# Attention and feed-forward in one kernel: weight chunks on another DMA queue, the first loads put in order, a scale found through DRAM

## The chip, the cores and the metric

The kernel runs on one core of a Trainium2 chip. A core has a matrix engine (TensorE, "PE" in the profile, with its weight loads listed apart as "PEld"), VectorE ("DVE"), ScalarE ("ACT"), GpSimd ("POOL") and SyncE ("SP"). Each engine takes its instructions from its own list, strictly in order, and waits on semaphores for the others. DMA transfers are issued by an instruction in the list of one of these engines (here of SP or of ACT) and are then carried out by the core's DMA engines. The metric is device time in microseconds (us); before the change its median over three runs is 1113.92 us.

## The reference

Attention for 8 batches of 8 heads, 576 positions, head width 64, and then a feed-forward layer over the 4608 rows that come out of it:

```python
scores = scale * q @ k.T                       # per head, 576 x 576
cum    = cumsum(maximum(s, 0))                 # s: one number per head and position
scores = where(causal, -1e9, scores + minimum(-(cum[:, None] - cum[None, :]), 0))
attn   = softmax(scores)
x      = attn @ v                              # 4608 rows of 512 after the heads are joined
h      = x @ w_in                              # 512 x 2048
g      = where(h >= 1, h, where(h <= -1, 0, (h + 1)**2 / 4))
out    = g @ w_out                             # 2048 x 512
```

All arrays are float32, except that the host hands over the two weight matrices as 64-bit words, which the kernel decodes.

## The kernel before, in words

**Numbers.** The feed-forward products run in float16 with each operand split in two halves (high and low), three products per pair. To stay in range, everything is scaled: for each batch `batch_scales_v` (L272) finds the largest absolute value of v over all heads (`m`, the same number on all 128 partitions), from which come `ex` (the factor with which the attention output px becomes the float16 tile x), and in `batch_scales` (L282) the factors us, ws, ub, gb of the feed-forward steps. Taking a maximum over partitions needs a detour: `column_max` (L94) transposes a column of 128 numbers on TensorE against the identity matrix `ident` into PSUM (`row_m`), VectorE takes its maximum (`top_m`); `spread` (L102) makes it bfloat16 and multiplies it with a row of ones on TensorE (`col_m`), and VectorE copies that to `mb`. Both PSUM tiles come from the two buffers (pool `ps_s`) that the score tiles s and the attention outputs px rotate through.

**Weights.** Each weight matrix comes in 16 chunks of 512 KB: `Weights.load` (L179) issues one into a raw buffer (wir for w_in, four buffers; wor for w_out, four buffers in two tags). `Weights.decode` (L192) turns it into float32: ScalarE L199, VectorE L200, a TensorE product with ones for the column sums (L204), then either ScalarE L212 and VectorE L213 or VectorE L215 and L216. The load of chunk c+3 stands behind the decoding of chunk c and waits until a raw buffer is free. After four chunks `scale` (L218) makes a factor and after all 16 `split` (L225) writes the float16 halves. `a_in` (L623), the bound over all of w_in, has to be there before the first wor chunk is loaded (it is copied into the buffer, L185) and before the factors of `batch_scales(0)`.

**Attention.** A job is a pair of heads with one half of the queries (half 0: 320 queries, half 1: 256). Per job: load q and k (QF/KF for the first eight jobs, rq/rk after; `att_load`, L319), scores per query tile (L411 to L417), bias, mask and minimum on VectorE (L422), exponentials on ScalarE (L433), then `weights_t` (L439): normalise and split on GpSimd, ScalarE and VectorE (L454 to L460) and transpose through a DMA issued by SP (`pt<-pb`, L461). `att_out` (L468) multiplies with the transposed v (`vt<-vb`, L392) into px (L479) and writes x (L490, L491). Scores of the next jobs run ahead of this.

**Feed-forward.** `ffn_h` (L527): twelve products per 128 columns (L534), then L546, L549, L550 on ScalarE and VectorE and the split of g (L560, L561). `ffn_y` (L565): twelve products per 128 rows of g (L573), and for the last of them the output. The feed-forward work of one batch is woven into the attention of the next (the loop at L644).

**Start.** Lines L601 to L629: load q and k of the first job, three wir chunks, v of batch 0 and the cumulative sums (`cum_out`, L155: `cumf`, `cumd` in DRAM), then 4 jobs of attention woven with 16 chunks to decode, then the factors, three wor loads and the splits. The feed-forward of batch 0 (h, then y) is woven with the decoding of wor.

**What sets the order.** The program is written in the order above, and a scheduler that works from a model of the instructions' times rearranges each engine's list. `tc.high_priority(offset)` moves a piece ahead by that many places; `tc.issue_after(i)` ties one instruction behind another. So a change at one place can move instructions everywhere. All loads of the inputs, all transposes and the cumulative sums are issued by SP (`nc.sync`); ScalarE's queue (`nc.scalar`) carries the outputs and the sums for later jobs (`Q<-cumd`, `K<-cumd`, L360, L361).

Of the kernel before, what the change touches and what calls it, by code (L numbers as in the profile page):

```python
# [7 lines left out]
BF16 = mybir.dt.bfloat16  # L8
F16 = mybir.dt.float16
F32 = mybir.dt.float32  # L10
# [5 lines left out]
ALU = mybir.AluOpType  # L16
AX = mybir.AxisListType.X
# [3 lines left out]
B, H, S, D = 8, 8, 576, 64  # L21
DM, DFF = 512, 2048
P = 128
# [23 lines left out]
START_LEAD = 20000  # L47
# [24 lines left out]
@with_exitstack  # L72
def attention_ffn(ctx: ExitStack, tc: tile.TileContext, qT, kT, vT, s, w_in, w_out, yT):
    nc = tc.nc
    LOADQ, CUMQ = nc.sync, nc.scalar
    V, A, G, T = nc.vector, nc.scalar, nc.gpsimd, nc.tensor

    cp = ctx.enter_context(tc.tile_pool(name="cp", bufs=1))
    ap = ctx.enter_context(tc.tile_pool(name="ap", bufs=2))
    gp = ctx.enter_context(tc.tile_pool(name="gp", bufs=2))  # L80
    dp = ctx.enter_context(tc.tile_pool(name="dp", bufs=1, space=DRAM))
    ps_s = ctx.enter_context(tc.tile_pool(name="ps_s", bufs=2, space=PSUM))
# [8 lines left out]
        V.tensor_scalar(out, in_, least, None, ALU.max)  # L91
        V.tensor_scalar(out.bitcast(I32), out.bitcast(I32), 0x7F800000, None, ALU.bitwise_and)

    def column_max(src, name):  # L94

        row = ps_s.tile([P, 512], F32, tag="s", name=f"row_{name}")
        T.transpose(row[:1, :P], src, ident)
        top = ap.tile([P, 1], F32, tag="top", name=f"top_{name}")
        V.tensor_reduce(top[:1], row[:1, :P], axis=AX, op=ALU.max)
        return top[:1]  # L100

    def spread(dst, top, name):  # L102

        t16 = ap.tile([P, 1], BF16, tag="t16", name=f"t16_{name}")
        V.tensor_copy(t16[:1], top)
        col = ps_s.tile([P, 512], F32, tag="s", name=f"col_{name}")
        T.matmul(col[:, :1], ones[:1], t16[:1], start=True, stop=True)
        V.tensor_copy(dst, col[:, :1])

    BH = B * H  # L110
    KC, KF32 = D + 4, D + 2
    NQ = HALF[0][1]
    QF, KF = [], []
    for i, (tq, tk) in enumerate((("rq", "rk"), ("q1", "k1"))):
# [2 lines left out]
    one = []  # L117

    st = ap.tile([P, S], F32, tag="vraw", bufs=4, name="st")
    nc.sync.dma_start(st[:BH], s)  # L120
    ch = ap.tile([P, 2, S], F32R, tag="raw", name="ch")
    zr = ch[:BH, 1].bitcast(F32)
    V.memset(zr, 0.0)
    V.memset(QF[0][D:KF32], 8.0)
    V.memset(KF[0][D:KF32], -8.0)
    V.tensor_scalar(st[:BH], st[:BH], 0.0, None, ALU.max)
    cum = ap.tile([P, S], F32, tag="raw", name="cum")
    V.tensor_tensor_scan(cum[:BH], st[:BH], zr, 0.0, ALU.add, ALU.add)
    cumf = dp.tile([BH, S], F32, name="cumf")
    cumd = dp.tile([BH, 2, S], F32, name="cumd")  # L130

    mask = cp.tile([P, S], F32, name="mask")
    G.memset(mask, 0.0)
    G.affine_select(
        out=mask, in_=mask, pattern=[[-1, S]], compare_op=ALU.is_ge,
        fill=-8.0 * BIG, base=448, channel_multiplier=1,
# [1 line left out]

    G.memset(QF[1][D:KF32], 8.0)
    G.memset(KF[1][D:KF32], -8.0)  # L140
    ident = cp.tile([P, P], F32, name="ident")
    G.memset(ident, 0.0)
    G.affine_select(
        out=ident, in_=ident, pattern=[[-1, P]], compare_op=ALU.not_equal,
        fill=1.0, base=0, channel_multiplier=1,
    )
    ones = cp.tile([P, P], BF16, name="ones")
    G.memset(ones, 1.0)

# [19 lines left out]
    class Weights:  # L169
# [9 lines left out]
        def load(self, n, after=None):  # L179
            if n < NW:  # L180
                c = self.order[n]
                pool, tag, bufs = self.tags[n % len(self.tags)]
                self.raw[c] = pool.tile([P, NC, 2], I32, tag=tag, bufs=bufs, name=f"{self.name}r{c}")
                if after is not None:
                    V.tensor_copy(self.raw[c][:, 0, :1], after.bitcast(I32))  # L185
                src = self.src(c)
                dst = self.raw[c]
                if len(src.shape) == 4:
                    dst = dst.rearrange("p (j n) t -> p j n t", j=2)
                nc.sync.dma_start(dst, src)  # L190

        def decode(self, n):  # L192
            c, g = self.order[n], n // self.size
# [45 lines left out]
    w1 = Weights(  # L239
        "wi", lambda c: w_in[c // 4 * P:(c // 4 + 1) * P, c % 4 * NC:(c % 4 + 1) * NC, :],  # L240
        WO, WI, ((gp, "g", G_BUFS),), [n % 4 * 4 + n // 4 for n in range(NW)], 4,
    )
# [15 lines left out]
    def load_v(b):  # L258
        for p in range(NPAIR):
            v = vraw[b, p] = ap.tile([P, S], F32, tag="vraw", bufs=4, name=f"v{b}_{p}")  # L260
            nc.sync.dma_start(v, vT[b, p])
# [10 lines left out]
    def batch_scales_v(b):  # L272
        t = ap.tile([P, 1], F32, tag="mt", name=f"mt{b}")
        V.tensor_reduce(t, csc[b], axis=AX, op=ALU.max)
        m = msc[b] = ap.tile([P, 1], F32, tag="mb", name=f"mb{b}")
        spread(m, column_max(t, f"m{b}"), f"m{b}")
        r = ap.tile([P, 1], F32, tag="mr", name=f"mr{b}")
        V.reciprocal(r, m)
        e = exs[b] = ap.tile([P, NPAIR], F32, tag="ex", name=f"ex{b}")
        V.tensor_scalar(e, csc[b], r, 2.0 ** -12, ALU.mult, ALU.mult)  # L280
# [212 lines left out]
    def batch_start(b):  # L493
        batch_v(b)
        if b:
            batch_scales_v(b)
# [101 lines left out]
            ffn_y(*ffn_q.pop(0))  # L598


    att_load(0, 0)  # L601
    for c in range(3):
        w1.load(c)
    load_v(0)
    cum_out()
    batch_start(0)
    for j in range(NPAIR):
        for k in range(8):
            if k % 2 == 0:
                c = 4 * j + k // 2  # L610
# [31 lines left out]
    t = 8 * NPAIR  # L642
    tasks = w2_tasks()
    for j in range(16 * NP):  # L644
# [14 lines left out]
        else:  # L659
# [3 lines left out]
            m = 2 * (j // 8 % 2)  # L663
# [36 lines left out]
```

## Time and profile before

| | |
|---|---|
| runs (3) | 1113.92 us median, 1113.88 to 1118.03 us |
| the profiled execution | 1117.59 us, of which the span of the profile is 1115.8 us |
| busy time | PE 1013.1 us (91%), DVE 843.6 (76%), ACT 731.0 (66%), POOL 637.1 (57%) |
| DMA | 155.09 MB, 139 GB/s over the span |
| weight chunks | 16 wir and 16 wor of 512 KB, all issued by SP |

How to read it: the profile is of one execution, 3.7 us longer than the median. In rows of a timeline the first number is the start in us from the span's start, the second the duration in us, then engine, line, operation and tiles; the bracket says how long the engine sat idle before it and what ended that. "SPq" and "ACTq" are DMA issues in SP's and ACT's lists. A row of the list of waits reads "engine line <- what it waited for: us in total, times, longest". The steady part of the kernel, from about 200 us on, is bound by TensorE; before that TensorE is busy about two thirds of the time.

### The profile page before, as it was taken

The page shows a single profiled execution, that of the slowest core. Times are in us where ns is not written, and L with a number is a line of the kernel's source. Part 1 is how long each engine was busy: PE and PEld are TensorE (multiplying, and loading weights), DVE is VectorE, ACT ScalarE, POOL GpSimd, SP SyncE. Part 2 cuts the span into 40 slices and gives each one's busy share as a digit, 9 for nine tenths or more (in the row PEclk, how much of TensorE's full clock was granted, in tenths as well). Part 3 has the DMA queues.
Part 4 walks back from the last instruction along what each step waited for, and adds up shares of the span by engine and source line. Part 5 has one row for each costly group of instructions (what it writes and reads, how often), then busy time and mean ns, then how long its engine had stood idle before and what let it go on. Part 6 is the DMA issues. An engine that isn't in the chain of part 4 may idle for free.

```text
span 1115.8 us, 24709 instructions
## 1 busy us (share of the span) xinstructions
PE 1013.1 (91%) x8495; PEld 777.3 (70%) x8496; DVE 843.6 (76%) x2327; ACT 731.0 (66%) x1711; POOL 637.1 (57%) x846
## 2 busy tenths in 40 slices
PE   3558788899999999899999999899988999999998
PEld 1224456687777877787777877687767877787787
DVE  6877895787777877787877887787777888887533
ACT  4856787677576765777576765677576756776432
POOL 3555667666456664566566655556467665666422
PEclk9967889899999999999999999999999999999999
DMA  6986864776387663878377764668379663776300
GB/s 222 213 190 178 177 143 103 157 153 153 83 166 164 150 139 84 190 156 152 83 160 163 147 136 84 169 147 165 68 159 181 145 145 80 162 155 126 67 25 20
DMA packets 340925, 155.09 MB, mean 139 GB/s; under 512 B 290984, under 2 KB 322572, under 8 KB 340800
## 3 DMA queue, kind: packets, MB, share of 16 engines
q1 hardware_dynamic: 331200, 143.68, 60.2%
q10 hardware_dynamic: 9600, 9.84, 2.7%
q8 instruction: 67, 1.10, 0.4%
q14 instruction: 58, 0.48, 0.1%
HBM read 72.28 MB, written 9.88 MB: 74 GB/s over the span
## 4 chain that ended last, share of the span: by engine, by line
PE 58%; DMA 12%; DVE 11%; POOL 8%; issue 6%; ACT 4%; SPq 1%; ACTq 0%; DVEq 0%; POOLq 0%
PE h L534 25%; PE y L573 23%; DMA pt<-pb 5%; PE px L479 4%; PE s L416 3%; PE s L417 3%; DMA wir<-in_moe_w_in_dram 2%; POOL pb L457 2%; POOL pb L454 2%; DMA vt<-vb 2%; DVE pb L460 2%; DVE PS L422 1%; POOL g L561 1%; DMA wor<-in_moe_w_out_dram 1%; DVE h L549 1%
## 5 line engine op out<-in xcount | busy, mean ns | idle before, releaser
L534 PE MATMUL h<-x,WI 128*128 128x256 f16 (+1 forms) x3072 | 462.8, 292 | 8.0 <-DVE u L550 6.2
L573 PE MATMUL y<-g,WO 128*128 128x256 f16 (+1 forms) x3072 | 451.0, 288 | 9.7 <-POOL g L561 7.3
L534 PEld LDWEIGHTS <-WI 128*128 128x128 f16 x3072 | 290.3, 100 | 106.0 <-issue 21.4
L573 PEld LDWEIGHTS <-WO 128*128 128x128 f16 x3072 | 287.8, 98 | 97.0 <-issue 18.6
L561 POOL TENSOR_TENSOR g<-u,g 128x320 f16<-128x320 f32 (+1 forms) x256 | 208.6, 815 | 175.8 <-ACT g L560 175.5
L433 ACT ACTIVATE PS<-PS,mn 64x64 f32<-64x64 f32 (+4 forms) x320 | 178.8, 559 | 131.4 <-DVE mn L422 114.3
L546 ACT ACTIVATE u<-h,ub,us 128x320 f32<-128x320 f32 (+1 forms) x256 | 148.8, 582 | 116.1 <-PE h L534 100.9
L454 POOL TENSOR_SCALAR pb<-PS,rs 64x128 f16<-64x128 f32 (+4 forms) x160 | 101.0, 631 | 207.1 <-DVE rs L450 136.1
L549 DVE SCALAR_TENSOR_TENSOR h<-h,ws,u 128x320 f32<-128x320 f32 (+1 forms) x256 | 132.3, 518 | 107.8 <-ACT u L546 106.5
L457 POOL TENSOR_TENSOR pb<-PS,pb 64x128 f16<-64x128 f32 (+4 forms) x160 | 168.0, 1050 | 11.5
L460 DVE SCALAR_TENSOR_TENSOR pb<-PS,rs,pb 64x128 f16<-64x128 f32 (+4 forms) x160 | 135.1, 845 | 49.6 <-POOL pb L454 49.0
L422 DVE CUSTOM_DVE_ANT_0 PS<-s,mask 64x64 f32<-64x64 f32 (+4 forms) x320 | 133.3, 419 | 26.3 <-PE s L417 23.4
L550 DVE SCALAR_TENSOR_TENSOR u<-u,r,h 128x320 f32<-128x320 f32 (+1 forms) x256 | 130.0, 508 | 6.6
L416 PE MATMUL s<-K,Q 128*64 128x64 f32 (+1 forms) x336 | 126.3, 378 | 6.2 <-DVE mn L422 2.6
L455 ACT ACTIVATE PS<-PS,rs 64x64 f32<-64x64 f32 (+4 forms) x160 | 88.9, 559 | 49.2 <-DVE rs L450 49.1
L560 ACT CAST g<-u 128x320 f16<-128x320 f32 (+1 forms) x256 | 107.9, 422 | 13.5 <-DVE u L550 13.4
L417 PE MATMUL s<-K,Q 68*64 68x64 f32 (+1 forms) x336 | 102.8, 309 | 7.2 <-POOL K L367 4.3
L479 PEld LDWEIGHTS <-vt 128*64 128x64 f16 x1536 | 73.5, 114 | 49.2 <-issue 37.2
L479 PE MATMUL px<-pt,vt 128*64 128x256 f16 (+3 forms) x1536 | 83.4, 259 | 23.7 <-DMA pt<-pb 20.9
L456 POOL TENSOR_SCALAR pb<-PS 64x128 f16<-64x128 f32 (+4 forms) x160 | 90.5, 566 | 21.0 <-ACT PS L455 19.0
L416 PEld LDWEIGHTS s<-K,Q 128*64 128x64 f32 (+1 forms) x336 | 61.5, 183 | 17.1 <-DVE mn L422 3.2
L417 PEld LDWEIGHTS s<-K,Q 68*64 68x64 f32 (+1 forms) x336 | 61.9, 185 | 9.5 <-POOL K L367 4.4
(108 smaller groups left out, 930.3 us busy)
## 6 DMA issues: line engine op xcount, KB each, us to landing
rk<-in_k_dram SPq DMA_DIRECT2D x56, 288.0 KB
v<-in_v_dram SPq DMA_DIRECT2D x32, 288.0 KB
rq<-in_q_dram SPq DMA_DIRECT2D x56, 160.0 KB
rk<-in_k_dram SPq DMA_DIRECT2D x56, 160.0 KB
wir<-in_moe_w_in_dram SPq DMA_DIRECT2D x16, 512.0 KB
wor<-in_moe_w_out_dram SPq DMA_DIRECT2D x16, 512.0 KB
rq<-in_q_dram SPq DMA_DIRECT2D x56, 128.0 KB
out_dram<-o ACTq DMA_DIRECT2D x32, 160.0 KB
```

The source lines that it names most:

```text
L416: T.matmul(sc[:R, :c1 - c0], Q1[:, hd, qo:qo + R], K1[:, hd, c0:c1], start=True, stop=False)
L417: T.matmul(sc[:R, :c1 - c0], Q2[:KC, hd, qo:qo + R], K2[:KC, hd, c0:c1], start=False, stop=True)
L422: ttr[0] = V.tensor_tensor_reduce(out=Pt[:R, c0:c1], in0=sc[:R, :c1 - c0], in1=mask[:R, mo:mo + c1 - c0], scale=-0.125 if j < F32_JOBS els ...
L433: A.activation(Pt[:R, :W], Pt[:R, :W], AF.Exp, bias=m2[:R], scale=-1.0, accum_out=sums[n, i][:R, hd:hd + 1])
L457: G.tensor_tensor(los[1], pw, his[1], ALU.subtract)
L460: V.scalar_tensor_tensor(los[0], pv, rs[:R, :1], his[0], ALU.mult, ALU.subtract)
L479: T.matmul(px[hd * D:(hd + 1) * D, lo:N], VT[:, vl * NB + j, hd * D:(hd + 1) * D], PT[:, 4 * j + 2 * hd + pl, lo:], start=(m == 0), stop=( ...
L534: T.matmul(h[:, :N], WI[4 * kt + ft // 4][:, wl, ft % 4 * P:(ft % 4 + 1) * P], x[:, kt, xl], start=(n == 0), stop=(n == 3 * NKT - 1),)
L546: first = A.activation(u, h[:, :N], AF.Relu, bias=ubi[b], scale=usc[b][:, fg:fg + 1]).ins
L549: V.scalar_tensor_tensor(h[:, :N], h[:, :N], wsc[b][:, fg:fg + 1], u, ALU.mult, ALU.max)
L561: G.tensor_tensor(g[:, 1], u, g[:, 0], ALU.subtract)
L573: T.matmul(ys[b, hf, m][:, :N], WO[8 * (m // 2) + ft // 2][:, wl, c0:c0 + P], g[:, gl], start=(ft == 0 and n == 0), stop=(ft == NFT - 1 an ...
```

## The change

Three edits, and what the scheduler makes of them.

```diff
@@ queue of the weight chunks
-    LOADQ, CUMQ = nc.sync, nc.scalar
+    LOADQ, CUMQ, WQ = nc.sync, nc.scalar, nc.scalar
...
-                nc.sync.dma_start(dst, src)
+                WQ.dma_start(dst, src)

@@ s, the sums, and first q, k put first
-    nc.sync.dma_start(st[:BH], s)
...
+    with tc.high_priority(offset=2 * START_LEAD):
+        nc.sync.dma_start(st[:BH], s)
+        V.memset(QF[0][D:KF32], 8.0)
+        zr = ch[:BH, 1].bitcast(F32)
+        V.memset(zr, 0.0)
+        V.memset(KF[0][D:KF32], -8.0)
+        V.tensor_scalar(st[:BH], st[:BH], 0.0, None, ALU.max)
+        V.tensor_tensor_scan(cum[:BH], st[:BH], zr, 0.0, ALU.add, ALU.add)
...
-    att_load(0, 0)
-    for c in range(3):
-        w1.load(c)
+    with tc.high_priority(offset=2 * START_LEAD):
+        for c in range(3):
+            w1.load(c)
+        att_load(0, 0)

@@ the largest value through DRAM (batch_scales_v)
         V.tensor_reduce(t, csc[b], axis=AX, op=ALU.max)
+        d = dp.tile([P], F32, name=f"md{b}")
+        nc.sync.dma_start(d.rearrange("(p o) -> p o", o=1), t)
+        a = ap.tile([P, P], F32, tag="ma", bufs=1, name=f"ma{b}")
+        nc.sync.dma_start(a, d.partition_broadcast(P))
         m = msc[b] = ap.tile([P, 1], F32, tag="mb", name=f"mb{b}")
-        spread(m, column_max(t, f"m{b}"), f"m{b}")
+        V.tensor_reduce(m, a, axis=AX, op=ALU.max)
```

`column_max`, `spread` and `ident` (a memset and an affine_select on GpSimd at the start) are gone. All 32 weight chunks are now issued from ScalarE's list. The column t of 128 numbers is written to DRAM (`md`) by one DMA of SP, read back by a second one as 128 equal rows (`ma`), and one VectorE maximum over each row gives `mb`.

**The start.** SP's list before, from its first load to the third wir chunk (lines of the kernel before; QF0/KF0 are q and k of the first job):

```order
L328 DMA QF1_79<-in_q_dram 64x2x320
L328 DMA KF1_80<-in_k_dram 64x2x320
L120 DMA st_81<-in_s_dram 64x576
L328 DMA QF0_77<-in_q_dram 64x2x320
L328 DMA KF0_78<-in_k_dram 64x2x320
L190 DMA wir0_161<-in_moe_w_in_dram 128x1024
L190 DMA wir4_163<-in_moe_w_in_dram 128x1024
L190 DMA wir8_165<-in_moe_w_in_dram 128x1024
```

After these rows come ten more DMAs (four rows of the sums, the four v, cumf, cumd), and only then the fourth chunk, wir12.

ACT's list now, from its first row (L169 is the changed kernel's line of the load, L178 and L191 are the decoding):

```order
L169 DMA wir0_150<-in_moe_w_in_dram 128x1024
L169 DMA wir4_152<-in_moe_w_in_dram 128x1024
L169 DMA wir8_154<-in_moe_w_in_dram 128x1024
L169 DMA wir12_190<-in_moe_w_in_dram 128x1024
L178 ACT_TABLE_LOAD
L178 ACTIVATE WO0_121<-wir0_150 128x512
L191 ACTIVATE wir0_150<-wir0_150,floor_bias_75 128x512
L178 ACTIVATE WO4_125<-wir4_152 128x512
L169 DMA wir1_202<-in_moe_w_in_dram 128x1024
```

Four chunks stand at the head of ACT's list where three stood behind five loads on SP, and the fourth no longer stands behind the ten DMAs. SP's list now begins with st, QF0, KF0, QF1.

**The first feed-forward step.** ACT's list around x of the fourth job (px3) and the first u (L546 before, L529 now). Before:

```order
L229 ACTIVATE WI15_125<-WO15_141,r_wi_145 128x512
L199 ACTIVATE WO2_128<-wor0_740 128x512
L490 ACTIVATE x0_0_440<-px3_0_699,ex0_297 128x320
L212 ACTIVATE wor0_740<-wor0_740,floor_bias_75 128x512
L199 ACTIVATE WO3_129<-wor1_743 128x512
L433 ACTIVATE PS512_151,sm0_3_852<-PS512_151,mn0_3_0_0_855 128x448
L199 ACTIVATE WO4_130<-wor2_746 128x512
L546 ACTIVATE u0_0_0_815<-h0_0_0_801,ub0_735,us0_731 128x320
```

Three wor chunks are begun ahead of the first u. Now, in the changed kernel's ACT list at the same place:

```order
L169 DMA wor9_912<-in_moe_w_out_dram 128x2x512
L178 ACTIVATE WO9_130<-wor7_854 128x512
L473 ACTIVATE x0_0_431<-px3_0_690,ex0_288 128x320
L178 ACTIVATE WO10_131<-wor8_861 128x512
L191 ACTIVATE wor8_861<-wor8_861,floor_bias_75 128x512
L178 ACTIVATE WO11_132<-wor9_912 128x512
L416 ACTIVATE PS512_146,sm0_3_843<-PS512_146,mn0_3_0_0_846 128x448
L529 ACTIVATE u0_0_0_806<-h0_0_0_792,ub0_726,us0_722 128x320
```

Before, one wor chunk is begun ahead of that x and three ahead of the first u; now eight (wor0 to wor7) and ten.

**The scale of a batch.** DVE's list at batch 3 in the changed kernel, from the column of maxima (mt) to the result (mb); L532 and L533 are the feed-forward steps (L549 and L550 before):

```order
L253 TENSOR_REDUCE mt3_5298<-c3_5288 128x1
L432 TENSOR_SCALAR rs11_4_5353<-sm11_4_5255 128x2
L249 TENSOR_SCALAR rc3_5289<-rc3_5289 128x4
L532 SCALAR_TENSOR_TENSOR h2_0_8_5412<-h2_0_8_5412,ws2_4447,u2_0_8_5426 128x320
L433 RECIPROCAL rs11_4_5353<-rs11_4_5353 128x2
L533 SCALAR_TENSOR_TENSOR u2_0_8_5426<-u2_0_8_5426,r2_4437,h2_0_8_5412 128x320
L405 ISA PS128_144,mn12_0_0_0_5451<-s12_0_0_0_5448,mask_92 64x64
L405 ISA mn12_0_0_0_5451 64x1
L474 SCALAR_TENSOR_TENSOR x2_1_4896<-px10_1_5360,ex2_3400,x2_1_4896 128x256
L443 SCALAR_TENSOR_TENSOR pb11_4_5352<-PS640_148,rs11_4_5353,pb11_4_5352 128x5x128
L259 TENSOR_REDUCE mb3_5304<-ma3_5302 128x1
L532 SCALAR_TENSOR_TENSOR h2_0_9_5456<-h2_0_9_5456,ws2_4447,u2_0_9_5469 128x320
```

Nine rows stand between mt and mb; before, eight stood there, among them `top_m` and its cast. In batch 1 it is four rows now, in batch 0 twenty-four.

More of the change, by code (lines that the diff above doesn't have):

```diff
@@ L92, in pow2floor @@
         V.tensor_scalar(out.bitcast(I32), out.bitcast(I32), 0x7F800000, None, ALU.bitwise_and)
[L94 to L108, printed above, removed]
     BH = B * H
@@ L119, in attention_ffn @@
     st = ap.tile([P, S], F32, tag="vraw", bufs=4, name="st")
-    nc.sync.dma_start(st[:BH], s)
     ch = ap.tile([P, 2, S], F32R, tag="raw", name="ch")
[L122 to L126, printed above, removed]
     cum = ap.tile([P, S], F32, tag="raw", name="cum")
-    V.tensor_tensor_scan(cum[:BH], st[:BH], zr, 0.0, ALU.add, ALU.add)
     cumf = dp.tile([BH, S], F32, name="cumf")
     cumd = dp.tile([BH, 2, S], F32, name="cumd")
+    with tc.high_priority(offset=2 * START_LEAD):
[6 more added lines that the diff above has]
+        V.tensor_tensor_scan(cum[:BH], st[:BH], zr, 0.0, ALU.add, ALU.add)
     mask = cp.tile([P, S], F32, name="mask")
@@ L140, in attention_ffn @@
     G.memset(KF[1][D:KF32], -8.0)
[L141 to L146, printed above, removed]
     ones = cp.tile([P, P], BF16, name="ones")
```

## The prediction

> **What bounds the kernel now.** I read the page first, then a table of stages, the waits and the chain of the start. The page says that TensorE is busy nine tenths of the time:
>
> ```profile
> span 1115.8 us, 24709 instructions
> PE 1013.1 (91%) x8495; PEld 777.3 (70%) x8496; DVE 843.6 (76%) x2327; ACT 731.0 (66%) x1711; POOL 637.1 (57%) x846
> ```
>
> That is a mean over two different stages. In the table of stages the columns are the stretch in us, its length, the busy time of PE, PEld, DVE, ACT and POOL (instructions behind an x), the granted TensorE clock, the DMA engines' busy share and GB/s:
>
> ```profile
> 0.00:20.00 20.00, 5.17 (x13) 2.40 (x13) 14.11 (x35) 7.34 (x12) 7.49 (x18) 1.00 0.80 242
> 20.00:60.00 40.00, 21.68 (x80) 10.61 (x80) 32.51 (x96) 32.29 (x68) 20.07 (x29) 1.00 0.78 192
> 60.00:90.00 30.00, 14.55 (x65) 8.46 (x66) 19.72 (x69) 14.85 (x34) 18.68 (x24) 0.53 0.88 217
> 130.00:160.00 30.00, 26.49 (x158) 15.90 (x157) 26.69 (x56) 28.33 (x54) 21.30 (x20) 0.90 0.80 170
> 200.00:1116.00 916.00, 881.05 (x7750) 697.19 (x7750) 693.91 (x1916) 594.47 (x1439) 522.44 (x708) 0.99 0.62 131
> 0.00:160.00 160.00, 99.37 (x473) 56.34 (x475) 126.68 (x336) 110.01 (x218) 86.74 (x109) 0.84 0.78 195
> ```
>
> From 200 us on TensorE is busy for 881 of 916 us (96%): what is saved on another engine there is worth nothing unless TensorE waits for it. In the first 160 us TensorE is idle for 60.6 us, VectorE for 33.3 and ScalarE for 50.0. The start is therefore where time can be found. What it waits for, over these 160 us:
>
> ```profile
> PE sum_wi L204 <- DVE WO L200: 24.3, 10, 10.4
> ACT WO L199 <- DMA wir<-in_moe_w_in_dram: 18.0, 7, 7.2
> DVE WO L200 <- ACT WO L199: 14.5, 11, 4.3
> PE px L479 <- DMA pt<-pb: 10.9, 3, 7.4
> ACT WO L199 <- DMA wor<-in_moe_w_out_dram: 8.8, 6, 3.4
> ```
>
> ScalarE waits 26.8 us for weight chunks, VectorE behind it 14.5 us, TensorE behind both. In the chain of waits of the first 100 us the longest DMA pieces say the same (start, length, what); the row of SP's timeline below them shows why the first is long:
>
> ```profile
> 13.62 8.25 DMA wir<-in_moe_w_in_dram
> 37.53 7.14 DMA pt<-pb
> 71.76 5.56 DMA wir<-in_moe_w_in_dram
> 84.68 4.44 DMA wor<-in_moe_w_out_dram
> ```
>
> ```profile
> 13.62 2.50 SPq L190 DMA_DIRECT2D wir<-in_moe_w_in_dram  x3
> ```
>
> The fourth chunk is issued only at 13.62 us, because SP's list has the sums and v ahead of it.
>
> **The change part by part.** *Start: queue and order.* Four chunks now head ACT's list, so the fourth comes some 12 us earlier, and later chunks no longer wait in SP's list behind transposes. The part of VectorE's idle time that wir chunks caused is one row of what waits for the tile wir:
>
> ```profile
>   DVE WO L200: 8.8, 7
> ```
>
> The other 5.7 of the 14.5 us are behind wor chunks. Can the DMA engines deliver earlier? From 0 to 90 us they are free for 0.20 x 20 + 0.22 x 40 + 0.12 x 30 = 16.4 us, so there is room for 8.8 us, not for much more.
>
> But the order costs something too. Three points of the start, the bound over w_in, x of the fourth job and the first feed-forward step on VectorE, with the durations of decoding (mean ns behind the busy time) and the stage table's row up to 109 us:
>
> ```profile
> 82.55 0.14 DVE L623 TENSOR_REDUCE a_in<-bound_wi 128x1 f32<-128x4 f32 x1
> 89.77 0.51 ACT L490 ACTIVATE x<-px,ex 128x320 f16<-128x320 f32 x1
> 93.79 1.07 DVE L549 SCALAR_TENSOR_TENSOR h<-h,ws,u 128x320 f32<-128x320 f32 x2
> L200 DVE TENSOR_SCALAR WO<-WO 128x512 int32<-128x512 int32 x31 | 15.9, 514 | 14.5 <-ACT WO L199 14.5
> L213 DVE SCALAR_TENSOR_TENSOR WO<-wor,WO 128x512 int32<-128x512 int32 x8 | 6.8, 850 | 1.6 <-ACT wor L212 1.6
> L216 DVE SCALAR_TENSOR_TENSOR WO<-wor,WO 128x512 int32<-128x512 int32 x7 | 5.9, 845 | 0.0
> L215 DVE SCALAR_TENSOR_TENSOR WO<-wor,WO 128x512 int32<-128x512 int32 x7 | 5.4, 771 | 0.0
> 90.00:93.80 3.80, 3.47 (x9) 1.77 (x9) 2.87 (x8) 3.80 (x8) 1.43 (x2) 0.50 0.24 93
> 90.00:109.00 19.00, 17.40 (x73) 9.89 (x73) 16.72 (x42) 15.30 (x29) 7.69 (x9) 0.76 0.43 140
> ```
>
> Ahead of that step VectorE's new list has seven more L200, three more L213 and four more each of L215 and L216: 3.6 + 2.6 + 3.1 + 3.4 = 12.6 us, with small ones 13. Before, VectorE had worked 66.3 + 2.9 = 69.2 us when it got there at 93.8 and had been idle 24.6. Now it has 82.2 us to do first; with 8.8 us less idle it gets there at 82.2 + 15.8 = 98.0. Later than before, but before, 82 us of work were reached only at 108 to 109 us (66.3 + 16.7 = 83.0 at 109). In work done the lead is 8.8 us, and up to 10. The weights allow it: 8.8 us less puts `a_in` at 73.8, or sooner since part of the fourth job's work now stands behind it; the first chunk takes 4.4 us, nine more at 0.52 MB and 217 GB/s take 2.4 each, which ends at 99.8, about the same time. I take **-7 us**: the 8.8, less some 2 us because x now stands behind eight chunks. Bounds: -14.5 (wor waits too) and +11 (rival C).
>
> *ScalarE issues the chunks.* Each issue takes, on SP, as a view of line L190 has it (min/median/max ns):
>
> ```profile
> L190 SPq DMA_DIRECT2D wir<-in_moe_w_in_dram x16: 357/392/1340, 4.1 to 71.8; - x16
> L190 SPq DMA_DIRECT2D wor<-in_moe_w_out_dram x16: 368/405/537, 84.7 to 150.8; - x16
> ```
>
> 16 x 0.39 + 16 x 0.41 = 12.8 us on ScalarE. It lies in ScalarE's 50 us of idle time, except where ScalarE is full (28.3 of 30 us at 130 to 160), where a few issues fall: **+1 us**; bounds 0 and 12.8 if that cover is gone. An issue also waits for VectorE to free its buffer, with exponentials behind it; in the new list the instruction behind nearly always waits for a later VectorE result anyway, so nothing for that.
>
> *The detour through TensorE goes.* Eight times (min/median/max ns):
>
> ```profile
> L97 PE MATMUL row_m<-ident,mt x8: 272/273/373, 20.3 to 920.6; 128*1 128x128 f32 x8
> L107 PE MATMUL col_m<-t_m,ones x8: 172/172/179, 25.0 to 924.1; 1*128 1x1 bf16 x8
> ```
>
> Seven of the eight are in the stage where TensorE is full: 7 x 0.445 = 3.1 us, **-3 us**. VectorE loses a reduction, a cast and a copy and gains a reduction: nothing. GpSimd's identity matrix goes from a time when GpSimd next waits for VectorE: nothing.
>
> *The trip through DRAM comes.* mb now follows mt by two DMAs in series. No row shows such a trip; the nearest are a DMA of 1.2 KB that TensorE waits for and the write of 144 KB to DRAM that the next load waits for. Beside them mt and mb before, in batch 2:
>
> ```profile
> 9.76 0.59 SPq L333 DMA_DIRECT2D KF<-cum  x1
> 12.42 0.58 PE L204 MATMUL sum_wi<-WO,ones 128*128 128x512 bf16 x1 [1.48 <-DMA KF<-cum]
> 12.44 0.50 SPq L156 DMA_DIRECT2D cumf<-cum  x1
> 16.80 0.68 SPq L336 DMA_DIRECT2D QF<-cumf  x1
> 296.60 0.12 DVE L274 TENSOR_REDUCE mt<-c 128x1 f32<-128x4 f32 x1
> 303.16 0.15 DVE L108 COPY mb<-col_m 128x1 f32<-128x1 f32 x1
> ```
>
> So 2.7 to 4.4 us each, 5.4 to 8.8 for two, against 6.6 us before. VectorE, with feed-forward and score steps queued behind mb, comes out between 1.2 us sooner and 2.2 us later at each of seven boundaries (batch 0's has 24 rows of cover); SP holds a transpose and loads of the next job behind ma. A gain I exclude, since TensorE's waits there do not name mb; the loss is at most 15 us. TensorE has h and y products queued, so I take a small part, nearest to the middle of the rows: **+2 us**. If the cover were gone it would be the 15.
>
> Sum: -7 + 1 - 3 + 2 = -7. The profiled execution took 1117.6 us (span 1115.8), which gives 1110.6; it was 3.7 us above the median, so the median should be **1107 us**.
>
> **The rivals.**
> *A, the transposes gain too.* The 7.14 us of the chain at 37.5 are a transpose behind 2 MB of weights on the same queue. On its own queue it would not stand behind them: half of the 10.9 us that px waits for pt goes as well, and the trip costs nothing: -8.8 - 5 - 3 + 1 = -16, 1098 us. For it: free DMA time; against: the same engines carry both, and weights could as well get ahead of the transposes. Chance 0.17.
> *B, the queue moves nothing.* The DMA engines are busy for 0.78 to 0.88 of the start, and a chunk that comes earlier makes q, k, v or a transpose later by as much; the wait changes its name. The start gives at most 1 us, and with -3, +1 and +2 the result is 1117.6 - 1 - 3.7 = 1113 us. Chance 0.22. The Trainium skill, "DMA: Bandwidth & Descriptors", section "Issuing engines are not separate DMA queues", says this as a rule: transfers from different issuers run on the same 16 engines and interleave, and issuing from several saves only the sequencer's time. The trace agrees as far as the shares go, but 13.62 us for the fourth chunk is an issue that comes late, which the rule leaves room for; that is why I do not put it first.
> *C, the first feed-forward step is late (slower).* On ScalarE x of job four waits behind eight wor chunks, u behind ten. If `a_in` stays near 82.6, the chunks end at 84.7 + 4.4 + 9 x 2.4 = 110.7, 17.6 us after the first u now (93.2); 12.6 us of decoding are then done ahead, so 5 us are lost, and at 3.4 us per chunk 14. With -3 + 1 + 2 that is +5 to +14: 1119 to 1128, say 1122 us. It decides if `a_in` comes after about 78 us. Chance 0.11.
> *D, the trip stalls VectorE (slower).* The 15 us in full on TensorE, with the start's gain: -7 + 1 - 3 + 15 = +6, 1120 us. Against it: TensorE's queue of products. Chance 0.05.
>
> **How the numbers follow.** Forecast 0.45, with a range of its own from 1102 to 1111; A 0.17, B 0.22, C 0.11, D 0.05. Some 0.5% (5.6 us) is what a measurement here can tell from no change. Faster than 1108.3: 0.31 of the forecast, A, and 0.04 of B, 0.52. Within: 0.14 of the forecast, 0.17 of B, 0.31. Slower than 1119.5: C, D and a little of B, 0.17. The range from 1097 to 1120 leaves out part of A below, and half of C and D above.
>
> **What would show it.** Right: the fourth wir chunk decoded by 16 us rather than 21.9; ScalarE's wait for wir under 10 us; `a_in` at 66 to 75; first u at 95 to 101; VectorE idle in the first 160 us down by about 7; wor finished some 20 us earlier; PE full from about 160. Wrong: `a_in` after 78 (B or C); ScalarE's waits for wor grown beyond 20 us (C); VectorE waiting over 2 us for ma at each boundary with TensorE idle beside it (D); TensorE's idle time after 200 us changed by more than 5 us either way, which a new order of the steady part could do and no term here holds.

## The result and the profile after

The changed kernel takes 1170.39 us (median of four runs, 1162.22 to 1178.9), beside 1114.27 us for the kernel before on the same chip: a ratio of 1.050, with a 95% interval from 1.045 to 1.055. 1107 us were forecast, so it is 56 us slower where 7 us less were expected. The profiled execution took 1178.9 us, 61 us more than that of before. TensorE's work is the same, spread over a longer span:

```profile
span 1177.1 us, 24685 instructions
PE 1014.8 (86%) x8480; PEld 775.7 (66%) x8480; DVE 833.7 (71%) x2311; ACT 733.5 (62%) x1711; POOL 632.3 (54%) x844
```

The table of stages, with the columns of before, and below it before's row for 100 to 160 us:

```profile
20.00:60.00 40.00, 10.83 (x42) 5.45 (x41) 25.55 (x79) 21.59 (x42) 13.19 (x17) 1.00 0.99 173
100.00:160.00 60.00, 34.76 (x165) 19.21 (x164) 42.04 (x90) 38.53 (x67) 25.64 (x28) 0.96 0.71 164
0.00:160.00 160.00, 71.45 (x297) 38.87 (x298) 109.81 (x287) 96.48 (x183) 69.32 (x89) 0.99 0.83 177
200.00:1116.00 916.00, 846.32 (x7400) 661.29 (x7398) 674.04 (x1913) 585.14 (x1421) 514.61 (x701) 0.96 0.62 134
```

```profile
100.00:160.00 60.00, 48.30 (x286) 29.67 (x286) 51.98 (x119) 47.40 (x91) 38.29 (x37) 0.89 0.81 185
```

The loss lies in both stages. In the first 160 us TensorE is busy for 71.5 us, 28 less than before (297 matmul records instead of 473). Of that, 10.9 us are lost from 20 to 60 us (10.8 against 21.7), where the DMA engines are busy all the time (0.99) and yet move less (173 GB/s; 0.78 and 192 before), and 13.5 us from 100 to 160 us, with 121 of the 176 missing records. From 200 to 1116 us TensorE is busy for 846 us, 35 less. The steady part has a wait that was not there, in the lists of waits of VectorE and of TensorE from 200 us on:

```profile
DVE mb L259 <- DMA ma<-md: 60.3, 7, 12.3
PE s L399 <- DVE mn L405: 34.5, 7, 8.5
```

One boundary, the last, in the timelines of VectorE, SP and TensorE (sorted by start):

```profile
968.50 0.13 DVE L253 TENSOR_REDUCE mt<-c 128x1 f32<-128x4 f32 x1
969.11 0.59 SPq L255 DMA_DIRECT2D md<-mt  x1
976.40 0.33 SPq L257 DMA_DIRECT2D ma<-md  x1
980.49 0.29 DVE L259 TENSOR_REDUCE mb<-ma 128x1 f32<-128x128 f32 x1 [7.75 <-DMA ma<-md]
981.41 0.53 PE L399 MATMUL s<-K,Q 128*128 128x192 f32 x1 [5.75 <-DVE mn L405]
982.22 2.56 SPq L444 DMA_TRANSPOSE pt<-pb  x1
```

The write of 128 numbers to DRAM takes 7.3 us (from md's issue to ma's, with only two other issues of SP between; 7.1 to 8.9 us at the seven boundaries), the read 4 us. mb is 12 us behind mt; VectorE has about 4 us of work to put between and stands for 7.8 us; the next scores stand behind it on TensorE.

The start, first in milestones (ScalarE's decoding of the fourth chunk, the bound over w_in, x of the fourth job, the first u), then the longer DMA pieces of the chain of waits up to 124 us (two of wir, at 51.65 and 63.01, are left out), and ScalarE's wait for wor chunks in the first 160 us:

```profile
13.60 0.69 ACT L178 ACTIVATE WO<-wir 128x512 f32<-128x512 f32 x1
L607 DVE TENSOR_REDUCE a_in<-bound_wi x1: 131/131/131, 80.4 to 80.4; 128x1 f32<-128x4 f32 x1
124.03 0.53 ACT L473 ACTIVATE x<-px,ex 128x320 f16<-128x320 f32 x1 [1.32 <-PE px L462]
127.58 0.59 ACT L529 ACTIVATE u<-h,ub,us 128x320 f32<-128x320 f32 x1
```

```profile
2.87 9.95 DMA QF<-in_q_dram
14.76 10.47 DMA cumf<-cum
32.09 12.57 DMA md<-mt
44.68 5.70 DMA ma<-md
81.52 13.09 DMA pt<-pb
98.51 3.83 DMA wor<-in_moe_w_out_dram
102.42 5.95 DMA wor<-in_moe_w_out_dram
108.53 4.34 DMA wor<-in_moe_w_out_dram
112.98 9.32 DMA wor<-in_moe_w_out_dram
ACT WO L178 <- DMA wor<-in_moe_w_out_dram: 21.9, 8, 7.0
```

The fourth chunk is there at 13.6 us instead of 21.9, as forecast. But the bound over w_in comes at 80.4 (82.5 before, 66 to 75 forecast), x of the fourth job at 124.0 (89.8) and the first u at 127.6 (93.2). SP's own transfers in the start are slow now: in the chain q of the second job takes 10 us, the sums 10.5 us, a transpose 13.1 us, and batch 0's trip through DRAM 18.3 us. What stands behind ma cannot leave SP's list before 44.7 us, among it a load of q and a transpose:

```profile
45.10 0.68 SPq L311 DMA_DIRECT2D QF<-in_q_dram  x1
47.95 1.21 SPq L444 DMA_TRANSPOSE pt<-pb  x1
```

From 98.5 us to x of the fourth job the chain is mostly four loads of wor chunks, 23.4 us together: eight of these chunks stand ahead of that x in ScalarE's list, and in the first 160 us ScalarE waits 21.9 us for wor chunks (8.8 before). This is the stretch from 100 us on in which most of the matmuls are missing.

### The profile page after: what moved, and what is told of

The parts are those of the page before. It is cut to its first block, busy times and chain, and to the rows that moved or that the text cites. A ratio compares the mean times of both kernels' runs of the same rounds, so it can differ in the third digit from the quotient of the medians.

```text
span 1177.1 us, 24685 instructions
## 1 busy us (share of the span) xinstructions
PE 1014.8 (86%) x8480; PEld 775.7 (66%) x8480; DVE 833.7 (71%) x2311; ACT 733.5 (62%) x1711; POOL 632.3 (54%) x844
## 4 chain that ended last, share of the span: by engine, by line
PE 49%; DMA 20%; DVE 15%; issue 5%; POOL 5%; ACT 4%; SPq 0%; ACTq 0%; DVEq 0%; POOLq 0%
PE h L517 21%; PE y L556 19%; DMA md<-mt 6%; DMA vt<-vb 4%; PE px L462 4%; DMA ma<-md 3%; PE s L399 3%; PE s L400 3%; DMA wor<-in_moe_w_out_dram 2%; POOL pb L437 2%; DVE PS L405 2%; DVE h L532 2%; DVE pb L443 2%; DMA pt<-pb 1%; DVE u L533 1%
## 5 line engine op out<-in xcount | busy, mean ns | idle before, releaser
L437 POOL TENSOR_SCALAR pb<-PS,rs 64x128 f16<-64x128 f32 (+4 forms) x160 | 105.9, 662 | 258.4 <-DVE rs L433 191.4
L532 DVE SCALAR_TENSOR_TENSOR h<-h,ws,u 128x320 f32<-128x320 f32 (+1 forms) x256 | 133.0, 520 | 100.2 <-ACT u L529 99.6
L529 ACT ACTIVATE u<-h,ub,us 128x320 f32<-128x320 f32 (+1 forms) x256 | 148.7, 581 | 84.1 <-PE h L517 73.9
L440 POOL TENSOR_TENSOR pb<-PS,pb 64x128 f16<-64x128 f32 (+4 forms) x160 | 165.2, 1033 | 12.0
L399 PE MATMUL s<-K,Q 128*64 128x64 f32 (+1 forms) x336 | 128.8, 385 | 39.6 <-DVE mn L405 34.5
L533 DVE SCALAR_TENSOR_TENSOR u<-u,r,h 128x320 f32<-128x320 f32 (+1 forms) x256 | 130.5, 510 | 7.5 <-DVE h L532 0.5
L439 POOL TENSOR_SCALAR pb<-PS 64x128 f16<-64x128 f32 (+4 forms) x160 | 88.0, 550 | 5.6 <-ACT PS L438 2.4
```

The source lines that it names most:

```text
L399: T.matmul(sc[:R, :c1 - c0], Q1[:, hd, qo:qo + R], K1[:, hd, c0:c1], start=True, stop=False)
L440: G.tensor_tensor(los[1], pw, his[1], ALU.subtract)
L529: first = A.activation(u, h[:, :N], AF.Relu, bias=ubi[b], scale=usc[b][:, fg:fg + 1]).ins
L532: V.scalar_tensor_tensor(h[:, :N], h[:, :N], wsc[b][:, fg:fg + 1], u, ALU.mult, ALU.max)
```

## The experiments

Each ratio is against the kernel before, run beside it; the interval is one of 95%.

### The three edits, each alone

The third edit alone (`batch_scales_v` of the changed kernel in the kernel before):

> The kernel before with the third edit alone: the largest value goes through DRAM, weight chunks and order as before. Theory 1 (the trip holds VectorE): each trip takes 12 to 13 us from mt to mb, VectorE waits about 8 us for ma at each of seven boundaries with feed-forward and score steps behind it, TensorE loses 5 us each: 35 to 40 us, 1149 to 1154 us. Theory 2 (the boundaries lose time because the changed order of the start shifts the steady part, and the wait for ma would be hidden by itself): within 8 us of before, 1106 to 1122 us. My prediction's term was +2 - 3, that is 1113 us.

Measured: 1155.42 us, ratio 1.037 (1.032 to 1.042). This is theory 1, a microsecond above its range. From 200 to 1105 us VectorE waits for ma as in the changed kernel, and TensorE for what VectorE then brings late:

```profile
DVE mb L258 <- DMA ma<-md: 47.2, 6, 8.2
PE s L398 <- DVE mn L404: 24.3, 4, 6.4
PE h L516 <- DVE u L532: 13.9, 3, 7.2
```

These two waits of TensorE make 38 us (2.6 and 2.0 us before).

The first edit alone, and the second:

```diff
-                nc.sync.dma_start(dst, src)
+                WQ.dma_start(dst, src)        # WQ = nc.scalar
```

> The kernel before with the first edit alone: weight chunks issued by ScalarE, order and scale as before. Theory 1 (the start loses 20 to 25 us because chunks on ScalarE's queue come in ahead of transposes and q, k, and because x and u stand behind wor chunks): 1130 to 1140 us, first u after 110 us, TensorE's busy time from 0 to 200 us down by 15 or more. Theory 2 (the start loses time because batch 0's trip holds SP's list from 32 to 50 us): 1105 to 1114 us, first u before 98 us.

> The kernel before with the second edit alone: s, sums, first q, k and three chunks at high priority, all on SP. Both theories: little, as the fourth chunk still stands in SP's list: 1109 to 1118 us. A rival (the order alone costs the start, since q and k now come behind other loads on SP and the scheduler's list is new): above 1120 us.

Measured: the queue 1126.37 us, ratio 1.012 (1.007 to 1.016); the order 1115.25 us, ratio 1.001 (0.998 to 1.004). The queue loses 11 us, less than theory 1 had and not the gain of theory 2, and its first u, at 102.0 us, lies between the two as well; the order loses nothing. Queue and order together, which is the changed kernel without the trip:

> The changed kernel without its third edit: the largest value by way of TensorE as before, chunks on ScalarE's queue and the new order kept. Theory 1 (start costs 20 to 25 of its own): 1130 to 1140 us, first u after 110 us. Theory 2 (the start's loss comes from batch 0's trip): 1105 to 1112 us. If the parts add, this and the trip alone give the sum of their differences, near +56.

Measured: 1125.62 us, ratio 1.011 (1.006 to 1.015): a loss of the start's own, but about half of what theory 1 had. The parts add: 3.7 + 1.2 + 0.1 = 5.0%, as measured for all three, within intervals of 0.3 to 0.5 each.

The loss of the queue is the instructive one, since with it alone nearly everything forecast of the start came true. The bound over w_in is there at 69.4 us, in the forecast's 66 to 75, and ScalarE's wait for wir is 3.5 us (18.0 before). The first 100 us of before, of the queue alone, and of queue and order (columns as above), then two milestones of the queue alone:

```profile
0.00:100.00 100.00, 51.07 (x189) 26.67 (x190) 74.70 (x218) 62.61 (x128) 48.45 (x72) 0.81 0.77 201
```

```profile
0.00:100.00 100.00, 46.00 (x169) 22.72 (x170) 83.08 (x216) 63.83 (x125) 50.26 (x71) 1.00 0.89 225
L623 DVE TENSOR_REDUCE a_in<-bound_wi x1: 139/139/139, 69.4 to 69.4; 128x1 f32<-128x4 f32 x1
98.10 0.51 ACT L490 ACTIVATE x<-px,ex 128x320 f16<-128x320 f32 x1
```

```profile
0.00:100.00 100.00, 39.76 (x143) 21.38 (x145) 79.28 (x211) 62.95 (x123) 43.64 (x71) 1.00 0.82 211
```

VectorE has worked 83.1 us by 100 us where it had worked 74.7: a lead of 8.4 us, and the forecast said 8.8. TensorE has worked 46.0 where it had worked 51.1, and 39.8 with the order too; since the granted clock differs (0.81 before, 1.00 here), its records say it better: 169 and 143 matmuls where there were 189.

That clock makes 74.7 a poor measure, though: in this one execution of before it was 0.53 from 60 to 90 us. The trip alone, with its chunks on SP as before, had 0.97 over the first 100 us:

```profile
0.00:100.00 100.00, 54.13 (x204) 28.21 (x205) 80.91 (x224) 63.92 (x132) 51.47 (x75) 0.97 0.81 201
```

The order alone and the DMA transpose alone (below), at 1.00, have 81.6 and 78.9 us of VectorE's work and 208 and 206 matmuls. Against these three the lead is only 1.5 to 4 us, and TensorE is 35 to 39 matmuls behind. The lead is decoding; the attention of the first four jobs, on which TensorE's next work hangs, comes later.

### What stands behind the trip

The trip alone, with mb, mr and ex moved 14 slots of the attention back:

```diff
-        V.tensor_reduce(m, a, axis=AX, op=ALU.max)    # in batch_scales_v, with mr and ex
+    def batch_scales_m(b): ...                        # the same three steps
...
+            if k == 3 and j > NPAIR and n % NPAIR == 1 and hf == 0:
+                with tc.issue_after(ttr[0]):
+                    batch_scales_m(n // NPAIR)
```

> The kernel before with the trip through DRAM alone, as in the run of the trip alone, but mb, mr and ex are computed 14 slots later (some 40 rows of VectorE behind mt rather than 10). Theory 1 (the loss is VectorE standing at mb with other work behind it): the trip itself still takes 12 us, VectorE's wait for ma falls from 47 to under 5 us, the time to 1108 to 1118 us. Theory 2 (the loss is SP standing at ma, which waits for md, with loads and transposes behind it): VectorE no longer waits for ma, but the time stays above 1130 us.

Measured: 1135.67 us, ratio 1.021 (1.015 to 1.028). Both theories hold in part: from 200 us on VectorE's list of waits has no ma any more, and less than half of the loss is gone. What is left stands on SP. Three of its rows at batch 4, and the waits from 200 to 1105 us, first of before and then of this kernel:

```profile
552.21 0.59 SPq L254 DMA_DIRECT2D md<-mt  x1
559.50 0.33 SPq L256 DMA_DIRECT2D ma<-md  x1
560.59 4.10 SPq L446 DMA_TRANSPOSE pt<-pb  x1
```

```profile
POOL vb L377 <- DMA vt<-vb: 36.8, 21, 3.4
DVE pb L460 <- POOL pb L454: 44.5, 56, 3.6
PE px L479 <- DMA pt<-pb: 7.4, 5, 2.7
```

```profile
POOL vb L362 <- DMA vt<-vb: 71.2, 24, 7.5
DVE pb L445 <- POOL pb L439: 81.1, 71, 8.1
PE px L464 <- DMA pt<-pb: 13.4, 7, 4.1
```

It is still 7.3 us from md's issue to ma's; two other issues fill the first 2, then SP stands for 5.3, and the transposes of the weights and of v wait behind: GpSimd's wait for vt is twice as long, VectorE's for GpSimd nearly so, TensorE's for pt too. The same delay in the changed kernel:

> The changed kernel with mb, mr and ex computed 14 slots later. Theory 1: it falls to the time of queue and order together, 1120 to 1130 us, or a few us above it, since in the start SP still stands at ma. Theory 2: above 1140 us.

Measured: 1157.29 us, ratio 1.037 (1.031 to 1.043): 13 us less than the changed kernel, theory 2's side. Then ma's issue moved back as well, behind the next transpose of v in SP's list:

```diff
+    def batch_scales_a(b):
+        a, d = mas[b]
+        with tc.issue_after(lastturn[0]):             # the last transpose of v
+            nc.sync.dma_start(a, d.partition_broadcast(P))
```

> The kernel before with the trip alone, mb 14 slots later as in the run with the late mb, and from batch 1 on ma's issue two transposes further behind in SP's list, so that md has landed when SP comes to it. Theory 1+2 (half of the loss was VectorE standing at mb, the other half SP standing 6 to 8 us at ma with transposes behind it): 1108 to 1120 us, GpSimd's wait for vt back from 71 to 35 to 45 us. Rival (the 20 us left come from something else, the list that the scheduler makes around a later mb): it stays above 1128 us.

> The changed kernel with the same two delays, in batch 0 too. If the trip costs only by those who stand behind it, what is left is the loss of queue and order: 1118 to 1130 us. Rival: above 1140 us, the chunks on ScalarE's queue make the trip itself longer.

Measured: 1123.11 us, ratio 1.007 (1.003 to 1.011), a little above what was expected, and in the changed kernel 1133.37 us, ratio 1.015 (1.011 to 1.019), between the two figures. So of the trip's 3.7% VectorE standing at mb makes 1.6, SP standing at ma 1.4, and 0.7 are left with neither standing, each figure some 0.4 to 0.8 either way and for this order of mending; the other order was not run. In this kernel GpSimd's wait for vt is still 54.9 us, not back at 35 to 45.

### Why the trip takes 12 us

md on the other queue, ma on SP's:

```diff
-        nc.sync.dma_start(d.rearrange("(p o) -> p o", o=1), t)
+        nc.scalar.dma_start(d.rearrange("(p o) -> p o", o=1), t)
```

> The trip alone again, mb as early as in the change, but md is issued on ScalarE's queue and only ma on SP's. If md is slow because it stands behind q and k on SP's queue, the time from md's issue to ma's falls from 7 to 8 us to 3 to 4, VectorE's wait for ma to about half, and the run to 1125 to 1140 us. If a write of 128 x 4 bytes to DRAM takes that long by itself, md to ma stays at 6 to 8 us and the run at 1148 to 1158 us.

```profile
428.85 0.35 ACTq L254 DMA_DIRECT2D md<-mt  x1
436.92 0.35 SPq L256 DMA_DIRECT2D ma<-md  x1
```

Measured: 1154.36 us, ratio 1.037 (1.034 to 1.041), and 8.1 us from md to ma: the queue is not the reason. That agrees with the Trainium skill, "DMA: Bandwidth & Descriptors", section "Issuing engines are not separate DMA queues": transfers of all issuers run on the same 16 engines.

Next the form of the write. 128 pieces of 512 bytes (each partition writes its number 128 times), 4 pieces of 128 bytes (VectorE turns the column into rows of 32 first), and 128 pieces of 4 bytes that lie 512 bytes apart:

```diff
+        V.tensor_copy(w, t.to_broadcast([P, 32]))     # 4 pieces
+        V.transpose(wt, w)
+        nc.sync.dma_start(d.rearrange("(g c) -> g c", c=32), wt[::32])
...
+        d = dp.tile([P, P], F32, name=f"md{b}")       # 128 pieces, 512 bytes apart
+        nc.sync.dma_start(d[:, :1], t)
```

> The trip alone with a write of 512 bytes per partition (64 KB) in place of 4 bytes, and a read of its first row only, so that the largest value is that of partition 0: the search over partitions is left out. If the 4-byte pieces make the write slow, the time from md's issue to ma's falls from 7 to 8 us to 3 to 4 us, and the run to 1125 to 1140 us. If a write to DRAM takes that long whatever its pieces, it stays at 6 to 8 us and the run near 1155 us.

> The kernel before with the trip alone, nothing late. VectorE first turns the column of maxima into rows of 32 (a copy and a 32 x 32 transpose, under 0.5 us), so that md is written as 4 pieces of 128 bytes in place of 128 pieces of 4 bytes; ma is read as in the change and the largest value is that of all partitions. If it is the 128 small pieces that make the write take 7 to 8 us, md's issue to ma's falls to 1.5 to 3 us, VectorE's wait for ma to 10 to 20 us, and the run to 1100 to 1115 us. If any piece under 512 bytes is slow, it stays at 6 to 8 us and the run at 1148 to 1158 us.

> The trip alone with md's 128 pieces of 4 bytes written 512 bytes apart in DRAM in place of side by side, and ma read back as the first of them alone, so that the largest value is that of partition 0: the search over partitions is left out. If the write is slow because the pieces share the same few bytes' neighbourhood in DRAM, the time from md's issue to ma's falls from 7 to 8 us to 2 to 3; if it is slow because each piece is 4 bytes, it stays at 6 to 9 us.

md's issue and ma's at batch 4, of the wide write, of the four pieces, and of the spread write:

```profile
533.59 0.60 SPq L256 DMA_DIRECT2D md<-mw  x1
536.22 0.33 SPq L258 DMA_DIRECT2D ma<-md  x1
```

```profile
539.01 0.56 SPq L258 DMA_DIRECT2D md<-mx  x1
541.28 0.35 SPq L260 DMA_DIRECT2D ma<-md  x1
544.12 0.29 DVE L262 TENSOR_REDUCE mb<-ma 128x1 f32<-128x128 f32 x1 [1.51 <-DMA ma<-md]
```

```profile
540.17 0.59 SPq L254 DMA_DIRECT2D md<-mt  x1
542.84 0.33 SPq L256 DMA_DIRECT2D ma<-md  x1
```

2.6, 2.3 and 2.7 us (2.4 to 3.7 for the spread write at batches 2 to 7; at batch 1 SP has a transpose to issue in between), against 7.7 at this batch in the change. Neither the number of pieces, nor their 4 bytes, nor pieces under 512 bytes are slow by themselves: 128 pieces of 4 bytes side by side are. The three took 1100.16 (one execution), 1111.44 (ratio 0.995, 0.993 to 0.998) and 1108.65 us (one execution). The four pieces keep the whole search, use mb as early as the change does, and are faster than before; VectorE's wait for ma is 12.2 us in place of 47.2 in the trip alone (200 to 1105 us), as expected.

### What the detour was worth, and both causes mended

No DRAM at all: the column as 128 equal bfloat16 columns goes through one DMA transpose of SP:

```diff
+        V.tensor_copy(w, t.to_broadcast([P, P]))      # bfloat16
+        nc.sync.dma_start_transpose(out=a, in_=w)
```

> The kernel before, with the detour through TensorE replaced by one DMA transpose: the column as 128 equal bfloat16 columns (the values are powers of two) is transposed by SP's queue into 128 equal rows, no DRAM and no second DMA. If the gain of the wide write (1100 us) came from the detour's end, and not from the part of the search that was left out there, this gives 1098 to 1110 us. If the -3 us of my prediction is all that the detour cost, 1110 to 1116 us.

> The changed kernel (queue and order kept) with the same DMA transpose in place of the trip. If the parts add: the gain or loss of the DMA transpose plus 10 us for queue and order, that is 1110 to 1125 us, against 1170 with the trip. If the chunks on the second queue slow transposes too, above 1130 us.

> Order and DMA transpose without the queue: chunks on SP as before, s and first q, k put first, the DMA transpose in place of the trip. Candidate for the fastest kernel: the order alone was worth nothing in the median (1115), so 1098 to 1112 us; it is below the DMA transpose alone if an early scale of batch 0 lets the order's lead of some 5 us of TensorE work in the first 200 us come through.

Measured: 1110.64 us, ratio 0.995 (0.992 to 0.998); in the changed kernel 1120.15, ratio 1.004 (1.002 to 1.007); with the order and without the queue 1110.04, ratio 0.994 (0.990 to 0.998). So the end of the detour through TensorE, with a quick way in its place, is worth 4 to 5 us, near the 3 of the prediction; the 1100 us of the wide write were one execution without the search over partitions, and no kernel with the whole search shows a gain of that size. In the changed kernel the transpose takes back 50 of the 56 us, and queue and order cost their 1% with or without a trip. The order adds nothing to the transpose that can be measured; these two and the four pieces are the kernels with the whole search that are faster than before, by half a per cent.

For the start, w_in's chunks alone on ScalarE's queue:

> The kernel before with w_in's 16 chunks on ScalarE's queue and w_out's 16 on SP as before. Theory B' (chunks that come early put decoding ahead of the attention of the first four jobs, and that is the loss): a_in at 65 to 72, x of the fourth job after 95, 1120 to 1130 us. Theory C' (the loss comes from ScalarE's list holding wor chunks and their waits ahead of x and u): first u before 96, 1108 to 1116 us.

Measured: 1123.51 us, ratio 1.008 (1.005 to 1.012): x of the fourth job at 102.4 us, the first u at 105.7. Time and x are in the ranges of theory B', so the issues of the wor chunks on ScalarE are not needed for the loss. But the decoding of these chunks stays in ScalarE's list: seven are begun ahead of that x (one before, seven with both matrices on the queue), so the run does not settle whether ScalarE's waits for them are part of the loss. Then decoding held back, with both matrices on ScalarE's queue:

```diff
+                with tc.issue_after(ttr[0]) if ttr[0] is not None else ExitStack():
                     w1.decode(c)
...
+                with tc.issue_after(ttr[0]):
                     w2.decode(c)
```

> Chunks on ScalarE's queue as in the run of the queue alone, but VectorE's steps of each decoding are tied behind the attention's last score step, so that 17 to 19 decodings stand ahead of x of the fourth job, as before the change, and not 23. Theory B' (the loss is decoding that goes ahead of attention in VectorE's list): back to 1108 to 1117 us, x of the fourth job at 85 to 92 us. Rival (the loss is the DMA engines: chunks run ahead of transposes and loads on another ring): 1121 to 1130 us as in the run of the queue alone.

Measured: 1119.26 us, ratio 1.004 (1.001 to 1.007): between the two ranges; two thirds of the queue's loss are gone, by the ratios. But x of the fourth job missed its figure:

```profile
95.27 0.53 ACT L490 ACTIVATE x<-px,ex 128x320 f16<-128x320 f32 x1 [1.49 <-PE px L479]
2.19 8.74 DMA st<-in_s_dram
```

It came at 95.3 us (98.1 without the tie, 89.8 before). The second row, from the chain, points to a part of the loss that stays: s, which everything in attention's first job needs, takes 8.7 us with four chunks in flight on the other queue (9.1 without the tie), and took 3.2 before. The tie also does more than one thing: three wor chunks are begun ahead of that x instead of seven, the first wor load goes from 70.2 to 83.3 us and the bound over w_in from 69.4 to 82.7. So the run shows that early decoding, with what comes along with it, makes most of the loss, but not which engine's list or which loads. Last, both causes mended in the changed kernel:

> The changed kernel with both causes mended: the DMA transpose in place of the trip, and VectorE's steps of each decoding tied behind attention's last score step (20 decodings ahead of x of the fourth job, not 23). If the two causes are the whole of the loss: 1120 less the 7 us that the tie gave with the queue alone, 1109 to 1116 us, the kernel before or a little better. If the order's early s, q and k add to it: below 1109. Rival (a third cause in the start): 1117 to 1123 us.

Measured: 1111.65 us, ratio 0.998 (0.995 to 1.001), in the range given for the case that the two causes are the whole of the loss. Beside the changed kernel with the DMA transpose but without the tie (ratio 1.004) the tie is worth 0.6%, some 7 us. Queue and order still gain nothing: the DMA transpose alone stands at 0.995.

## Why the prediction was wrong, step by step

**The trip through DRAM (+2 us, at most 15): failed.** This term decided the result. Against a trip that takes little (the DMA transpose, -0.5%) it costs 3.7 + 0.5 = 4.2%, some 47 us. Three things were wrong in it.

- The size of the write. 2.7 to 4.4 us per DMA came from a load of 1.2 KB and a write of 144 KB. The read kept to it (4 us); the write of 128 pieces side by side took 7.1 to 8.9 us, and no row of before showed such a write.
- The price of the wait. I took 6.6 us before against 5.4 to 8.8 after and priced the difference. Yet in the 6.6 us VectorE was mostly at work on the eight rows between (from 200 us on it stood 4.4 us at mb in all); with 12 us it runs out of rows and stands for nearly 8. The wait is the length of the trip less the work that can be put in between, not the difference of two trips. The argument that TensorE has h and y products queued failed with it: h waits for u of VectorE, and the scores for mn, and both stand behind mb.
- SP. The prediction named what SP holds behind ma and gave it no price. It is about as dear as VectorE's wait (1.4 against 1.6 of the 3.7%, mended in this order).

Rival D had the mechanism, and its test came true (over 2 us of waiting for ma at each boundary, with TensorE idle beside), but it stood at 15 us and a chance of 0.05.

**The start (-7 us): failed, on another step than the ones doubted.** The fourth chunk, the wait for wir and the bound over w_in came as said when the queue was changed alone. The lead in VectorE's work, 8.4 us for 8.8, did so partly by luck: it is measured against an execution with half the clock from 60 to 90 us, and is 1.5 to 4 us against kernels at 0.97 to 1.00. The step that failed is "In work done the lead is 8.8 us", taken as a lead in time. It was a lead in decoding. Work of one kind done early on an engine that serves two chains is not a lead for the chain that TensorE waits for: VectorE was 1.5 to 8 us ahead, by the execution it is measured against, and TensorE 20 to 39 matmuls behind. In the changed kernel itself even the bound over w_in came late. Batch 0's trip, for which I had looked only at VectorE's "24 rows of cover", held back q, k and transposes in SP's list; with the DMA transpose in its place the bound still came only at 82 us, so that the trip alone does not explain this milestone.

**ScalarE's issues (+1), the detour (-3): not contradicted.** w_in alone on ScalarE's queue loses as much as both matrices within the intervals, so the 16 issues of wor show no cost, but intervals of 4 us either way could not show 1 us. The detour's end, with a quick way in its place, is worth 4 to 5 us, 2 to 9 by the interval.

**The rivals.** B said that what comes earlier makes something else later by as much; for s with the queue alone that is what the rows show (3.2 to 9.1 us), but B's price was no loss. C named the right place (x and u behind eight and ten chunks), and both its signs came true in the changed kernel: the bound over w_in at 80.4 us, after 78, and ScalarE's wait for wor at 21.9 us, over 20. Its price for the start, +5 to +14, contains the 10 us of queue and order. Only its condition was too narrow: x comes late, behind seven to nine chunks, with the bound at 65 to 69 us too. So C and D happened together, where the prediction had them as alternatives, with 0.11 and 0.05. A did not occur: the chain of the changed kernel has a transpose of 13.1 us.

**What stays open.** Why writes that lie side by side are slow; what the 0.7% are that the trip costs when neither engine stands at it; how the queue's loss divides between VectorE's list, ScalarE's wor chunks and slow loads such as that of s, which the tie does not separate; and why the bound over w_in comes at 80 to 82 us in the changed kernel and in its version with the DMA transpose, but at 65 us with queue and order alone.

## What to carry to other kernels

Price a wait in an in-order list by its whole length less the work ahead of it, and do it for every engine that stands, the one that issues the transfers included; a dependent pair of DMAs on one queue stops all transfers behind it until the first has landed, here for some 5 us each time. Work that comes early helps only if it is work of the chain that the bottleneck waits for: ask of a lead which kind of work it consists of, and look at the granted clock of the profile that it is measured against. A column of single numbers that must cross partitions took 11 to 13 us from mt to mb as 128 places side by side in DRAM, 6 to 10 as four rows, and 4 to 5 by one DMA transpose (batches 2 to 7).

## What the runs showed of the hardware

A write of 512 bytes from 128 partitions into 128 neighbouring 4-byte places takes 7.1 to 8.9 us at the boundaries of the changed kernel (6.2 to 10.5 in the other kernels in which ma follows it at once), three times as long as the same pieces 512 bytes apart (2.7 us), 128 times the bytes in pieces of 512 (2.6 us), or the same bytes in four pieces (2.3 us; all these with SP's own work between the two issues). The Trainium skill, "DMA: Bandwidth & Descriptors", section "Latency and other measured facts", has a fixed cost of about 2 us per DMA; the three quick forms are near that, the slow one is not. The section "Why small descriptors are slow (HBM only)" names costs per piece, which would be the same for pieces side by side and apart, so they do not explain the difference.

With four chunks of 512 KB issued on ScalarE's queue from 0.7 us on, the load of s (144 KB) that SP issues at 2.2 us takes 9.1 us instead of 3.2: the second queue did not keep the two apart. In the changed kernel, where SP issues s first, at 0.7 us, VectorE has it at 6.4 us (5.4 before).
